# Slab 0's first weight columns tile by tile, gate and up in one slot: the head of a fused scan-and-GEGLU kernel re-ordered

## The chip, the cores and the metric

The kernel runs on one core of one Trainium2 chip. The metric is the device time of one execution in microseconds (us). Seven runs of the kernel before gave a median of 184.31 us, from 183.27 to 184.84: 183.27, 183.41, 183.49, 184.31, 184.45, 184.56 and 184.84. One execution was taken by the profiler; its own time was 183.49 us, and its span, from the first to the last instruction, 181.7 us.

Engines are called as the profile calls them: PE is the matrix engine, PEld its weight loads, DVE the vector engine, ACT the scalar engine, POOL the GpSimd engine, SP the sync engine. A "q" behind a name is that engine's DMA queue. An engine takes its instructions in the order in which the program lists them, and an instruction that waits holds up all those behind it on its engine.

## The reference, cut to what matters

```python
xn = layernorm(x)                               # x: 2048 tokens x 512
# branch A: a diagonal complex recurrence over the tokens
Lam_bar = exp(dt * Lam);  B_bar = ((Lam_bar - 1) / Lam)[:, None] * Bmat
h_t = Lam_bar * h_(t-1) + B_bar @ xn_t          # 512 complex states
s   = 2 * Re(h @ Cmat.T) + xn * Dskip
# branch B: gated feed-forward, 512 -> 1376 -> 512
g   = silu((gelu(xn @ w_gate) * (xn @ w_up)) @ w_down)
out = x + s * g
```

Inputs, weights and output are bfloat16.

## The kernel before, in words

The 2048 tokens are cut into four slabs of 512, each slab into four tiles of 128 (M = 4). The 1376 gate and up columns are cut into three chunks of 512, 512 and 352 (`CH`). PSUM is used as three slots of two banks (`slots[0..2]`, taken in turn by `slot()`) and two single banks (`ybank`).

Per slab the work is: layer norm of four tiles (`stats`, `rstd`, `norm_dve`: DVE makes the statistics, POOL the power -1/2, DVE the scaled tile `xn`); a transposition of `xn` to `xnT`; gate and up products on PE, moved out of PSUM by ACT (Gelu for gate, Copy for up) and multiplied on DVE into `at`; `half` twice (the products with B on PE, moved out by ACT into `U`, and then rotation, scan and back-rotation on DVE into `hst`); `down_pair` twice (the products with `w_down`); and `y_tile` four times (the products with C, then the end of the formula on DVE and a store).

Slab 0 is special. Its four tiles are transposed on PE through `ybank` and moved out by ACT (`head_t`, L642, `transposed`, L345), while later slabs use transposing DMAs (`dma_t`, L373). Its chunk 0 is done by `first_chunk` (L405): first the gate products of tiles 0 to 3 into two slots, then the up products of tiles 0 to 3 into two slots; ACT moves two tiles at a time (1024 columns). Chunks 1 and 2 of slab 0 use `gate_pair` (L384): one tile's gate and up share one slot, and ACT moves 512 or 352 columns at a time.

Before the first product, the program does the following. ACT's queue loads three small vectors of 512 (`pv0` = log_dt, `pv1` = Lambda_im, `pv2` = Lambda_re; L273) and then the gate weights of chunk 0. SP's queue loads the four x tiles, then the up weights of chunk 0, and chunk 1 and the rest. POOL's queue loads `Drow` (the row of Dskip). PE runs eight matmuls on a constant tile (`dummies`, L339), then `parameters` (L629): four tiny matmuls that turn `pv1`, `pv2`, `dt` and `dt*Lambda_im` into columns, and one that spreads `Drow` over 128 partitions, both into slot 2. ACT copies the spread row back (L637) and DVE copies the columns to `pf` (L638); since both share a slot, each waits for both. `tables` (L594) makes angles from `pf` on DVE (L598 to L602), their sines and cosines on ACT (L603, L604, then small copies on ACT and POOL, L606, L607) and the products of them on DVE (L618), from which the rotations are made.

The order on each engine is not written by hand. Each step is given to `Plan` (L23) with a cost, a lag until its result is seen elsewhere, what it reads and writes, and a rank. `Plan.run` (L113) makes a list schedule, repeats it with changed priorities, keeps the one with the best value, and then emits the steps in the order of their planned starts. PE's steps keep the order in which they were added. The plan only sets the order; the chip's time comes from the real waits.

Of the kernel before, what the change touches and what calls it, by code (L numbers as in the profile page):

```python
# [18 lines left out]
LOOK, HOLD, TABLE, ROUNDS, TRIALS = 0.3, 8.0, 6.0, 6, 1200  # L19
# [3 lines left out]
class Plan:  # L23
# [88 lines left out]

    def run(self):  # L113
        n = len(self.steps)
        deps = [s[3] for s in self.steps]
        users = [[] for _ in range(n)]
        for i in range(n):
            for d in deps[i]:
                users[d].append(i)
        tail = [0.0] * n  # L120
        for i in range(n - 1, -1, -1):
            eng, cost, lag = self.steps[i][0], self.steps[i][1], self.steps[i][4]
            tail[i] = cost + max((tail[u] + (0.0 if self._same(i, u) else lag) for u in users[i]), default=0.0)
        rank = [s[7] for s in self.steps]
        rng = random.Random(1)
        best = None
        prio = tail
        self.lengths = []
        work = [i for i in range(n) if self.steps[i][0] == PE]
        for r in range(ROUNDS + TRIALS):  # L130
            if r >= ROUNDS:
                lo = rng.uniform(-10.0, rng.choice((20.0, 170.0)))
                hi = lo + rng.choice((10.0, 25.0, 60.0))
                share, size = rng.choice((0.1, 0.3)), rng.choice((0.5, 2.0, 6.0))
                prio = [p + (rng.gauss(0.0, size) if lo <= t <= hi and rng.random() < share else 0.0) for p, t in zip(best[2], best[1])]
            key = [p + q for p, q in zip(prio, rank)]
            start, length = self._pass(deps, key, True)
            goal = length + 0.5 * sum(start[i] for i in work) / len(work)
            self.lengths.append(round(length, 1))
            if best is None or goal < best[0]:  # L140
                best = (goal, start, prio)
            if r < ROUNDS:
                back, _ = self._pass(users, [start[i] + self.steps[i][1] for i in range(n)], False)
                prio = [back[i] + self.steps[i][1] for i in range(n)]
        start = best[1]
        self.start = start
        for i in sorted(range(n), key=lambda i: (start[i], i)):
            self.steps[i][2]()
# [3 lines left out]
def kernel(  # L152
# [119 lines left out]
    for i, v in enumerate((A_log_dt, A_Lambda_im, A_Lambda_re)):  # L272
        dma_first(ACT, 0.45, 2.5, lambda i=i, v=v: nc.scalar.dma_start(out=pv[i][:], in_=v.rearrange("(k p) -> k p", p=P)),  # L273
            [("pv", i)], not_before=0.72)
    for m in range(M):
        dma_first(SP, 0.45, 1.75 + 0.12 * m, lambda m=m: nc.sync.dma_start(out=x_tok[:, m, :], in_=x_r[:, m, :]), [("x", 0, m)], not_before=0.72)
    load_w(dma_first, ACT, nc.scalar, 0, (0.47, 3.9), 0)
    for c, which, land in ((0, 1, 3.3), (1, 0, 3.1), (1, 1, 2.9)):
        load_w(dma_first, SP, nc.sync, c, (1.45, land), which)
    dma_first(SP, 1.45, 2.7, lambda: nc.sync.dma_start(out=x_tok[:, M : 2 * M, :], in_=x_r[:, M : 2 * M, :]), [("x", 1, m) for m in range(M)])  # L280
    for ri, src in enumerate((A_B_re, A_B_im)):
        dma_first(SP, 2.4, 2.7, lambda ri=ri, src=src: nc.sync.dma_start_transpose(out=BT[:, ri, :, :], in_=src), [("BT", ri)])
    for which in range(2):
        load_w(dma_first, SP, nc.sync, 2, (1.0, 2.7), which)
    ident = sb("ident", [P, P])
    id4 = sb("id4", [4, 4], FP32)
    pool(0.8, lambda: make_identity(nc, ident[:]), writes=["ident"], rank=190.0)
    dma(POOL, 0.7, 2.2, lambda: G.dma_start(out=Drow[0:1, :], in_=A_Dskip.rearrange("(a d) -> a d", a=1)), writes=["Drow"], rank=200.0)
# [18 lines left out]
    dve(128, lambda: V.tensor_tensor(out=pr[1][:], in0=pv[1][:], in1=pr[0][:], op=ALU.mult), [("pv", 1), "dtr"], ["thr"], base=0.13, rank=150.0)  # L307
# [37 lines left out]
    def transposed(src, n, dst, reads, writes, bank, evict):  # L345
        tp = ybank[bank][:].bitcast(BF16)[:, 0:D].rearrange("p (k t) -> p k t", t=P)

        def f():
            for k in range(KT):
                T.transpose(tp[:, k, :], src[:, k * P : (k + 1) * P], ident[:])  # L350
        pe(KT, P, f, reads + ["ident"], [("y", bank)])
        if evict == ACT:
            acts(512, lambda: act(out=dst, in_=tp, func=AF.Copy), [("y", bank)], writes, rank=40.0)
        else:
            dve(512, lambda: V.tensor_copy(out=dst, in_=tp), [("y", bank)], writes, rate=2.0, rank=40.0)
# [17 lines left out]
    def dma_t(s, m):  # L373
        c0 = (s % 2) * TS + m * P
        return dma(SP, 1.2, 1.3, lambda: nc.sync.dma_start_transpose(out=xnT[:, :, c0 : c0 + P], in_=xn[m][:]),
            [("xn", m)], [("xnT", s % 2, m)])
# [5 lines left out]
    gu_n = [0]  # L382

    def gate_pair(s, m, c):  # L384
# [9 lines left out]
        for bank, (nm, wt) in enumerate((("wg", wg), ("wu", wu))):  # L394
            def f(bank=bank, wt=wt):
                for k in range(KT):
                    T.matmul(ps[:, bank, 0:w], lhsT=xnT[:, k, t0 : t0 + P], rhs=wt[:, k, a:b], start=(k == 0), stop=(k == KT - 1))  # L397
            pe(KT, w, f, [("xnT", s % 2, m), (nm, c)], [("slot", i, bank)])
        both = [("slot", i, 0), ("slot", i, 1)]
        gd, ud = gt[qb][:, qo : qo + w], ub[qb][:, qo : qo + w]  # L400
        acts(w, lambda: act(out=ud, in_=ps[:, 1, 0:w], func=AF.Copy), both, [("ub", q)])
        acts(w, lambda: act(out=gd, in_=ps[:, 0, 0:w], func=AF.Gelu_apprx_tanh), both, [("gt", q)], table="gelu")
        dve(w, lambda: V.tensor_tensor(out=at[j][:, a:b], in0=gd, in1=ud, op=ALU.mult), [("gt", q), ("ub", q)], [("at", j, c)], rate=2.0)

    def first_chunk(between):  # L405

        w = CH[0][1]
        for nm, wt, dst, ring, fn in (("wg", wg, gt, "gt", AF.Gelu_apprx_tanh), ("wu", wu, ub, "ub", AF.Copy)):
            for h in range(2):
                i, ps = slot()  # L410
                for b in range(2):
                    m = 2 * h + b

                    def f(m=m, b=b, ps=ps, wt=wt):
                        for k in range(KT):
                            T.matmul(ps[:, b, :], lhsT=xnT[:, k, m * P : (m + 1) * P], rhs=wt[:, k, 0:w], start=(k == 0), stop=(k == KT - 1))  # L416
                    pe(KT, w, f, [("xnT", 0, m), (nm, 0)], [("slot", i, b)])
                    between(nm, m)
                both = [("slot", i, 0), ("slot", i, 1)]
                kw = {"table": "gelu", "after": early} if nm == "wg" else {}  # L420
                acts(2 * w, lambda ps=ps, dst=dst, fn=fn, h=h: act(out=dst[h][:, 0 : 2 * w].rearrange("p (b w) -> p b w", b=2), in_=ps[:, :, :], func=fn),
                     both, [(ring, 2 * h), (ring, 2 * h + 1)], **kw)
        for m in range(M):
            o = (m % 2) * w
            dve(w, lambda m=m, o=o: V.tensor_tensor(out=at[m][:, 0:w], in0=gt[m // 2][:, o : o + w], in1=ub[m // 2][:, o : o + w], op=ALU.mult),
                [("gt", m), ("ub", m)], [("at", m, 0)], rate=2.0)
# [165 lines left out]
    early = []  # L592

# [35 lines left out]
    def parameters():  # L629
        pt_ps = slots[2][:, 0, 0:16]  # L630
# [4 lines left out]
        pe(4, 150, f, [("pv", 1), ("pv", 2), "dtr", "thr", "ident", "id4"], [("slot", 2, 0)])  # L635
        pe(1, 512, lambda: T.matmul(slots[2][:, 1, :], lhsT=warm[0:1, 0:P], rhs=Drow[0:1, :], start=True, stop=True), ["Drow", "warm"], [("slot", 2, 1)])
        acts(512, lambda: act(out=Drow[:], in_=slots[2][:, 1, :], func=AF.Copy), [("slot", 2, 0), ("slot", 2, 1)], ["Drow"], rank=50.0)  # L637
        dve(16, lambda: V.tensor_copy(out=pf[:], in_=pt_ps), [("slot", 2, 0), ("slot", 2, 1)], ["pf", "thn", "dt"], rank=10.0)  # L638
# [5 lines left out]

    dummies(8, 0)
    parameters()
    dummies(2, 0)
# [5 lines left out]
    dummies(1, 1)  # L653
    head_t(1)

    def between(nm, m):
        if nm == "wg" and m + 2 < M:
            head_t(m + 2)
        if nm == "wg" and m == 0:
            tables()  # L660

    first_chunk(between)
    dma_first(SP, 3.6, 2.7, lambda: nc.sync.dma_start(out=wd[:, 0 : NFT - 1, :], in_=B_w_down[0 : (NFT - 1) * P, :].rearrange("(k p) d -> p k d", p=P)), ["wd"])
    dma_first(SP, 0.4, 2.7, lambda: nc.sync.dma_start(out=wd[:FL, NFT - 1, :], in_=B_w_down[(NFT - 1) * P : F, :]), ["wd"])
# [84 lines left out]
    for ri, src in enumerate((A_C_re, A_C_im)):  # L749
        dma(SP, 2.4, 2.7, lambda ri=ri, src=src: nc.sync.dma_start_transpose(out=CT[:, ri, :, :], in_=src),  # L750
# [69 lines left out]
```

## Time and profile before

| | |
|---|---|
| time, median of 7 runs (range) | 184.31 us (183.27 to 184.84) |
| time of the profiled execution; its span | 183.49 us; 181.7 us |
| PE busy | 174.7 us (96%) |
| DVE busy | 158.4 us (87%) |
| ACT busy | 118.2 us (65%) |
| POOL busy | 10.5 us (6%) |
| first gate matmul of slab 0 starts | 8.61 us |
| first matmul of chunk 1 starts | 16.41 us |
| last matmul ends, by the chain | 177.65 us |

The page gives, for one execution, the busy time of each engine, the chain of work that ended last, the costliest groups of instructions and the DMA issues. The chain is followed back from the last instruction, at each step to what released it. A timeline lists instructions in order of time: start, length, engine, line, operation, output and input; in brackets is the idle time of the engine before it and what ended that. A group in a timeline ("x4") runs from the start of its first to the end of its last. Ends of matmuls are modelled: four matmuls that are issued 0.22 us apart show as 1.03 us, because the last one is still draining while the next group has started.

### The profile page before, as it was taken

What the parts mean: (1) busy time and instruction counts of PE and PEld (TensorE: products, weight loads), DVE (VectorE), ACT (ScalarE), POOL (GpSimd) and SP (SyncE); (2) the same over time, 40 slices, a digit from 0 to 9 for tenths busy, and PEclk for the clock granted to TensorE, in tenths of its full rate; (3) what the DMA queues carried; (4) which work ended last, traced back from release to release, by engine and by line L of the source; (5) the groups of instructions that cost most, each with busy time, mean ns of one, the idle gap of its engine ahead of it and who ended that gap; (6) DMA issues with size and microseconds to landing.
All of it is one profiled execution on the core that took longest, in us unless ns stands there. A gap on an engine that the chain in (4) does not pass through costs nothing.

```text
span 181.7 us, 2385 instructions
## 1 busy us (share of the span) xinstructions
PE 174.7 (96%) x850; PEld 82.5 (45%) x850; DVE 158.4 (87%) x264; ACT 118.2 (65%) x174; POOL 10.5 (6%) x21
## 2 busy tenths in 40 slices
PE   6799999999999999999999999999999999999990
PEld 2444445544444545444444544544444545444440
DVE  5689999999999999999999999999999999740072
ACT  4578699799999899747349954527618666352220
POOL 4334002000000200000020000000000000000000
PEclk9999999999999999999999999999999999999998
DMA  4999999994000459500022470441100175720011
GB/s 116 370 316 227 356 125 209 283 192 106 0 0 0 87 101 140 108 0 0 19 69 61 94 141 10 79 79 61 39 21 0 23 89 92 146 81 8 0 58 58
DMA packets 46995, 18.01 MB, mean 99 GB/s; under 512 B 38440, under 2 KB 46984, under 8 KB 46984
## 3 DMA queue, kind: packets, MB, share of 16 engines
q1 hardware_dynamic: 46400, 17.34, 44.5%
q10 hardware_dynamic: 552, 0.53, 1.0%
q8 instruction: 6, 0.10, 0.2%
q14 instruction: 5, 0.04, 0.1%
q0 software_dynamic: 32, 0.00, 0.0%
HBM read 6.33 MB, written 2.10 MB: 46 GB/s over the span
## 4 chain that ended last, share of the span: by engine, by line
PE 54%; DVE 35%; ACT 6%; issue 3%; DVEq 0%
PE slot L440 18%; PE ybank L502 11%; PE slot L483 10%; DVE Fs L575 10%; DVE Q L556 9%; PE slot L542 6%; PE slot L397 4%; PE slot L342 2%; PE slot L416 2%; DVE C L758 2%; DVE at L458 1%; DVE hst L564 1%; DVE hst L568 1%; DVE C L755 1%; DVE sk L379 1%
## 5 line engine op out<-in xcount | busy, mean ns | idle before, releaser
L440 PEld LDWEIGHTS <-xnT 128*128 128x128 bf16 x288 | 28.1, 98 | 28.7 <-issue 0.3
L483 PE MATMUL slot<-wd,atT 128*128 128x512 bf16 (+1 forms) x176 | 38.7, 379 | 0.0
L440 PE MATMUL slot<-wg,xnT 128*128 128x512 bf16 (+1 forms) x144 | 31.8, 357 | 0.1
L440 PE MATMUL slot<-wu,xnT 128*128 128x512 bf16 (+1 forms) x144 | 31.8, 357 | 0.0
L575 DVE TENSOR_TENSOR_SCAN Fs<-rho,ini,W 128x512 bf16<-128x512 f32 x24 | 29.4, 1268 | 0.0
L502 PE MATMUL ybank<-C,hst 128*128 128x512 bf16 x128 | 28.8, 379 | 0.0
L542 PE MATMUL slot<-xnT,BT 128*128 128x512 bf16 x128 | 28.3, 379 | 0.0
L483 PEld LDWEIGHTS <-atT 128*128 128x128 bf16 (+1 forms) x176 | 17.2, 97 | 20.9
L545 ACT ACTIVATE U<-slot 128x1024 bf16<-128x1024 f32 x16 | 16.2, 1020 | 10.4 <-PE slot L542 10.2
L508 DVE TENSOR_TENSOR yg<-ybank,g 128x512 bf16<-128x512 f32 x14 | 9.6, 688 | 14.4 <-PE ybank L502 13.9
L542 PEld LDWEIGHTS <-BT 128*128 128x128 bf16 x128 | 12.5, 98 | 15.0
L502 PEld LDWEIGHTS <-hst 128*128 128x128 bf16 x128 | 12.5, 98 | 14.3
L556 DVE TENSOR_TENSOR Q<-U,tab 128x4096 bf16<-128x4096 bf16 x8 | 18.3, 2289 | 0.2
L556 DVE TENSOR_TENSOR Q<-Fs,tab 128x4096 bf16<-128x4096 bf16 x8 | 18.3, 2289 | 0.2
L498 ACT ACTIVATE ybank<-sk 128x512 f32<-128x512 bf16 x14 | 8.4, 601 | 15.2 <-DVE yg L508 14.7
L487 ACT ACTIVATE g<-slot 128x1024 f32<-128x1024 f32 x8 | 8.2, 1023 | 14.2 <-PE slot L483 14.1
L448 ACT ACTIVATE ub<-slot 128x1024 bf16<-128x1024 f32 x12 | 12.3, 1024 | 3.4 <-PE slot L440 3.4
L448 ACT ACTIVATE gt<-slot 128x1024 bf16<-128x1024 f32 x12 | 12.3, 1024 | 2.8 <-PE slot L440 2.8
L732 ACT ACTIVATE junk<-x_tok 128x512 bf16<-128x512 bf16 x16 | 10.0, 628 | 0.2
L575 DVE TENSOR_TENSOR_SCAN Fs<-rho,W 128x512 bf16<-128x512 f32 x8 | 9.4, 1209 | 0.0
L397 PEld LDWEIGHTS <-xnT 128*128 128x128 bf16 x64 | 6.3, 98 | 5.6
L458 DVE TENSOR_TENSOR at<-gt,ub 128x1024 bf16<-128x1024 bf16 x12 | 8.1, 677 | 0.0
(117 smaller groups left out, 183.8 us busy)
## 6 DMA issues: line engine op xcount, KB each, us to landing
out_dram<-ot SPq DMA_DIRECT2D x16, 128.0 KB, 1.7
x_tok<-in_A_x_dram SPq DMA_DIRECT2D x3, 512.0 KB, 7.2
wd<-in_B_w_down_dram SPq DMA_DIRECT2D x1, 1280.0 KB
wu<-in_B_w_up_dram SPq DMA_DIRECT2D x2, 512.0 KB
x_tok<-in_A_x_dram SPq DMA_DIRECT2D x4, 128.0 KB, 2.9
wg<-in_B_w_gate_dram ACTq DMA_DIRECT2D x1, 512.0 KB, 4.9
wg<-in_B_w_gate_dram SPq DMA_DIRECT2D x1, 512.0 KB, 6.5
wg<-in_B_w_gate_dram SPq DMA_DIRECT2D x1, 352.0 KB, 3.9
```

Of the source, the lines that this page charges most:

```text
L397: T.matmul(ps[:, bank, 0:w], lhsT=xnT[:, k, t0 : t0 + P], rhs=wt[:, k, a:b], start=(k == 0), stop=(k == KT - 1))
L440: T.matmul(ps[:, bank, 0 : b - a], lhsT=xnT[:, k, t0 : t0 + P], rhs=wt[:, k, a:b], start=(k == 0), stop=(k == KT - 1))
L448: acts(1024, lambda ps=ps, dst=dst, fn=fn: act(out=dst[:, 0:1024].rearrange("p (c w) -> p c w", c=2), in_=ps[:, :, :], func=fn), [("slot", ...
L458: dve(1024, lambda: V.tensor_tensor(out=at[j][:, 0:1024], in0=gt[q][:, 0:1024], in1=ub[q][:, 0:1024], op=ALU.mult), qs[0] + qs[1], [("at", ...
L483: T.matmul(ps[:, b, :], lhsT=atT[:fs, k, m * P : (m + 1) * P], rhs=wd[:fs, k, :], start=(k == 0), stop=(k == NFT - 1))
L502: T.matmul(bank[:, :], lhsT=hst[s % 2][:, j // NPT, j % NPT, m * P : (m + 1) * P], rhs=C2[:, j // NPT, j % NPT, :], start=(j == 0 and not ...
L508: dve(512, lambda: V.tensor_tensor(out=yg[e][:], in0=bank[:], in1=g2[gi][:, b, :], op=ALU.mult), [("y", i), ("g2", gi)], [("yg", e)])
L542: T.matmul(ps[:, ri, :], lhsT=BT[:, ri, k, pt * P : (pt + 1) * P], rhs=xnT[:, k, (s % 2) * TS : (s % 2 + 1) * TS], start=(k == 0), stop=(k ...
L545: acts(1024, lambda q=q, ps=ps: act(out=U[ui][:, :, q, :], in_=ps[:, :, :], func=AF.Copy), [("slot", i, 0), ("slot", i, 1)], [("U", ui, q)])
L556: dve(4096, lambda: V.tensor_tensor(out=Qf, in0=src.unsqueeze(1).to_broadcast(WQ), in1=table, op=ALU.mult), reads, ["Q"], rate=2.0)
L575: pl.add(DVE, 1.116 if s == 0 else 1.19, lambda ri=ri, q=q, pt=pt, first=first: V.tensor_tensor_scan(out=Fs[:, ri, q, :], data0=rho[:, pt ...
L732: acts(512, lambda i=i, fn=fn, m=m: act(out=junk[:], in_=x_tok[:, s * M + m, :], func=fn, accum_out=sx[:, s, i, m : m + 1]), [("x", s, m)] ...
```

## The change

In short: (1) `first_chunk` is gone. Chunk 0 of slab 0 is done by `gate_pair` like chunk 1: tile by tile, gate and up of a tile in one slot, moved out by ACT 512 columns at a time. The transpositions of tiles 1, 2 and 3 are put between these products: tile 1's behind gate 0, tile 2's behind up 0, tile 3's behind up 1. (2) `parameters` and the spreading of `Drow` (now `spread`) come behind the first transposed tile on PE instead of ahead of it, and write to slot 1 and slot 2, so that their copies no longer wait for each other. (3) Three of the eleven dummy matmuls are gone (the eight first ones stay). (4) `pv1` and `pv2` are loaded on POOL's queue instead of ACT's. (5) The assumed landing times of DMAs and some ranks are changed, and the planner has another search: `_decode` builds a schedule from a list of start times, and 3000 trials shift those. This changes the order on DVE and ACT in all of the kernel's first 100 us.

The order of the instructions that follows for each engine: PE: eight dummies, transposition 0, parameters, spread, gate 0, transposition 1, up 0, transposition 2, gate 1, up 1, transposition 3, gate 2, up 2, gate 3, up 3; from chunk 1 on as before. ACT, from its eighth instruction on: `xnT` of tile 0, `Drow`, `xnT` of tile 1, sine, copy, cosine, copy, `ub` 0, `xnT` of tile 2, the Gelu table, `gt` 0, `xnT` of tile 3, and then `ub`, `gt` of tiles 1, 2, 3. POOL: `Drow`'s load, the identity, the loads of `pv1` and `pv2`, the index rows (iota), three powers (tiles 0 to 2), two copies for the tables, the power of tile 3. DVE: statistics of tiles 0 and 1, `xn` 0, `dt*Lambda_im`, statistics of tile 2, `xn` 1, `pf`, three steps of the angles, `xn` 2, the fourth, statistics of tile 3, two products with `Drow`, `xn` 3. The set of DVE instructions ahead of the first rotation (L556 on `U0`) is the same in both. Further on, DVE makes slab 2's `sx` steps and `nb` (L737 to L743) ahead of two DVE steps of `y_tile` and three products with `Drow`, where they came behind them.

```diff
-    for i, v in enumerate((A_log_dt, A_Lambda_im, A_Lambda_re)):
-        dma_first(ACT, 0.45, 2.5, lambda i=i, v=v: nc.scalar.dma_start(out=pv[i][:], in_=v.rearrange("(k p) -> k p", p=P)),
-            [("pv", i)], not_before=0.72)
+    load_p(0, A_log_dt)
+    load_w(dma_first, ACT, nc.scalar, 0, (0.47, 4.5), 0)
...
+    for i, v in ((1, A_Lambda_im), (2, A_Lambda_re)):
+        dma(POOL, 0.7, 2.0, lambda i=i, v=v: G.dma_start(out=pv[i][:], in_=v.rearrange("(k p) -> k p", p=P)), writes=[("pv", i)], rank=220.0 - i, not_before=1.2)
...
-    def gate_pair(s, m, c):
+    def gate_pair(s, m, c, then=((), ())):
...
             pe(KT, w, f, [("xnT", s % 2, m), (nm, c)], [("slot", i, bank)])
+            for t in then[bank]:
+                head_t(t)
...
     def parameters():
-        pt_ps = slots[2][:, 0, 0:16]
+        pt_ps = slots[1][:, 0, 0:16]
...
-        pe(4, 150, f, [("pv", 1), ("pv", 2), "dtr", "thr", "ident", "id4"], [("slot", 2, 0)])
-        pe(1, 512, lambda: T.matmul(slots[2][:, 1, :], lhsT=warm[0:1, 0:P], rhs=Drow[0:1, :], start=True, stop=True), ["Drow", "warm"], [("slot", 2, 1)])
-        acts(512, lambda: act(out=Drow[:], in_=slots[2][:, 1, :], func=AF.Copy), [("slot", 2, 0), ("slot", 2, 1)], ["Drow"], rank=50.0)
-        dve(16, lambda: V.tensor_copy(out=pf[:], in_=pt_ps), [("slot", 2, 0), ("slot", 2, 1)], ["pf", "thn", "dt"], rank=10.0)
+        pe(4, 150, f, [("pv", 1), ("pv", 2), "dtr", "thr", "ident", "id4"], [("slot", 1, 0)])
+        dve(16, lambda: V.tensor_copy(out=pf[:], in_=pt_ps), [("slot", 1, 0)], ["pf", "thn", "dt"])
...
+    def spread():
+        pe(1, 512, lambda: T.matmul(slots[2][:, 1, :], lhsT=warm[0:1, 0:P], rhs=Drow[0:1, :], start=True, stop=True), ["Drow", "warm"], [("slot", 2, 1)])
+        acts(512, lambda: act(out=Drow[:], in_=slots[2][:, 1, :], func=AF.Copy), [("slot", 2, 0), ("slot", 2, 1)], ["Drow"])
+
     dummies(8, 0)
-    parameters()
-    dummies(2, 0)
...
     head_t(0)
-    dummies(1, 1)
-    head_t(1)
...
-    first_chunk(between)
+    parameters()
+    spread()
+    tables()
+    for m in range(M):
+        gate_pair(0, m, 0, (((1,), (2,)), ((), (3,)), ((), ()), ((), ()))[m])
```

## The prediction

> **What bounds the kernel now.** I read first the waits of PE, over the whole span; each line is: who waited for whom, us in total, times, longest.
>
> ```profile
> PE slot L342 <- DVE junk L297: 1.6, 1, 1.6
> PE ybank L350 <- DVE xn L369: 0.7, 1, 0.7
> PE slot L416 <- ACT gt L421: 0.3, 1, 0.3
> PE slot L416 <- ACT xnT L353: 0.2, 1, 0.2
> ```
>
> All of them lie before 15 us. From the first matmul of chunk 1 (16.41 us in the timeline) PE works without a hole that matters. I checked it by counting: 312 matmuls of 512 columns at 0.216 us (L542: 16 in 3.47 us) and 64 of 352 at 0.149 us (L397: 4 rows start 0.595 us apart) make 76.9 us, and 16.41 + 76.9 is 93.3, where slab 2's first gate matmul starts (93.33). So a change of the head can only move the time by what it moves chunk 1's start, plus stalls removed or made behind it. Second, the chain, in order of time, gives the head and the one later stall (start, length, what):
>
> ```profile
> 6.34 0.61 ACT Drow L637
> 6.97 0.17 DVE pf L638
> 7.14 0.33 DVE xn L369
> ...
> 7.52 0.41 PE ybank L350 x4
> 7.95 0.61 ACT xnT L353
> ...
> 8.61 1.04 PE slot L416 x4
> ...
> 12.31 1.28 ACT L421
> 13.61 1.03 ACT gt L421
> 14.68 1.89 PE slot L416 x8
> 16.57 6.91 PE slot L397 x32
> ...
> 95.07 0.81 ACT xn L714
> 95.90 1.28 ACT L448
> 97.20 1.03 ACT gt L448
> 98.27 4.81 PE slot L440 x24
> ```
>
> The reader sees the detour that the change removes: the first scaled tile waits on DVE behind `pf`, and `pf` behind the copy of `Drow`. At 98.27 PE had run out of work at 97.98 (4 up matmuls from 97.38, 0.149 each) and waited 0.29 us for a Gelu, which waited for a table, which waited for `xn`, which waited for `nb` on DVE. Third, busy time by stage: from 28.02 to 98.27 DVE is as full as PE.
>
> ```profile
> 28.02:98.27 70.25, 70.12 (x347) 33.79 (x346) 69.49 (x113) 56.75 (x90) 2.61 (x3) 1.00 0.45 87
> ```
>
> The columns are stage, length, then busy us and instructions of PE, PEld, DVE (69.49 of 70.25), ACT, POOL. A PE that starts earlier must find DVE earlier too.
>
> **The head, step by step.** POOL comes first, since the power for tile 0 now stands behind two more DMA issues. Rows of POOL:
>
> ```profile
> 1.21 0.73 POOL L288 DMA_DIRECT2D Drow<-in_A_Dskip_dram  x1 [0.78 <-POOLq L804]
> 2.60 0.18 POOL L289 CAST id<-ident 4x4 f32<-4x4 bf16 x1
> 2.74 0.15 POOL L312 IOTA iota_i<- 128x32 int32 x1
> 3.10 0.36 POOL L314 TENSOR_SCALAR iota_f<-iota_i 128x49 f32<-128x49 int32 x1
> 4.70 1.11 POOL L332 TENSOR_TENSOR rs<-ve,mhalf 128x1 f32<-128x1 f32 x2 [1.24 <-DVE mv L329]
> ```
>
> An issue of such a load on POOL is seen once, 0.73 us; two from 2.78 to 4.24, index rows 0.72 more (2.74 to 3.46 before), so the power runs 4.96 to 5.51 (0.55 each). The statistics of tile 0 are no obstacle (2.89 + 0.69 + 0.18 + 0.15, done at 3.96). `xn` 0: 5.56 to 5.96, against 7.06 to 7.46. The two issues are thus on the path; on ACT's queue such issues took 0.25 and 0.32. Bounds for the pair: 0.57 and 1.46; I take 1.46, the same queue. Drow's load landed 2.4 us after its issue began, so `pv2` lands at about 5.9; the slowest load in the head, 512 KB of x, took 7.8 us, which is the far bound.
>
> PE: transposition 0 at 6.02 (0.06 after `xn`, as before); its next group starts 0.23 us later; parameters and spread took from 5.09 to 6.23, 1.14 us, so gate 0 starts at 7.40 (its `xnT` is out at 7.07: ACT 0.60; gate weights landed 4.9 us after issue, so at about 6.3). Against 8.61 that is 1.2 us earlier. But ACT gives half of it back. Transposition 1 runs 8.27 to 8.66. ACT, with the start-to-start distances of the same rows: `xnT` 1 from 8.71 (0.50), sine (0.39), copy (0.22), cosine (0.48), copy (0.22), `ub` 0 at 10.52 (0.50), `xnT` 2 at 11.02 to 11.62, Gelu table 11.64 (1.28, +0.02), `gt` 0 at 12.94 (0.50), `xnT` 3 at 13.44 to 14.04. PE beside it: up 0 to 9.36, transposition 2, gate 1 and up 1 from 9.60 to 11.33; tile 3 waits for `xn` 3 (its power stands on POOL behind the two copies, the second from 10.30; 0.37 + 0.55, then DVE 0.40: 11.7), so transposition 3 at 11.75; gate 2 and up 2 from 12.0 to 13.72; gate 3 waits for `xnT` 3 and starts at 14.08; up 3 ends 15.81. Chunk 1 starts at **15.81 instead of 16.41: -0.60 us**. Its slot is free: `gt` 1 ends at 14.95.
>
> Costed at nothing: the three dummies (0.61 + 0.38 us of rows) lie in PE's waits for `xn` and `xnT`; the eight 512-wide evictions instead of four 1024-wide ones (0.50 x 8 against 1.03 x 4) run under chunk 1; the up weights, now needed at 8.5 instead of 12.5: by 6 us the load on SP's ring had moved 0.58 MB, of which 0.52 are x, so 0.46 MB is left at 370 GB/s and it ends near 7.3 to 7.9. If that cover of 0.6 us fails, each us costs a us.
>
> A rule of the Trainium skill speaks against the removed dummies. Row first: the eight dummies went at 0.45 us each, the spread at 5.93 took 0.37 us, which is the fast form; so PE's pace doubled between 5.16 and 5.93, while the granted clock in the stage rows stands at 1.00 throughout. "TensorE: Matmul & The Clock Gate", section "What's actually happening", says that the pace is set by how busy PE was in a free-running window of about 3.4 us. By it the hole from 5.16 to 6.02 might put off the fast form by a window in some executions; by the page's figure an estimate would be about 0.9 us more. No row here shows it.
>
> **Behind the head.** The same DVE set stands ahead of the first rotation. Its wait is ACT's `U`: ACT's last eviction of chunk 1 ends near 23.8, then a table copy (1.87) and two `U` (0.93, 1.02) make 27.6 instead of 28.02: DVE gains 0.4, PE 0.6. The tightest place behind it: `y_tile` 3 of slab 0 started at 75.19 and its bank was seeded at 75.00 (`ybank` L498, 74.40 + 0.60); this slack of 0.19 takes up the difference of 0.2. At 98 the order helps: `sx` comes ahead of two `y_tile` steps (0.35 and 0.69), so `nb` comes about 0.9 us earlier beside its 0.4, ACT's `xn` starts straight behind the Silu, and the Gelu ends 97.1 where PE needs its slot at 97.4. **-0.29 us**. From there PE is dense to 177.65 in both, and the tail is unchanged. Sum: -0.60 - 0.29 = -0.89. Against the profiled execution's own 183.49 that is 182.6; that execution lies 0.82 below the median of 184.31, to which the runs after will be compared, so **183.4**.
>
> **The rivals.** (A) *The gain is eaten.* DVE stays where it was, since `U` hangs on ACT's table copy, and PE waits for it at `y_tile` 3 and again at 98. For it: DVE's 99% between 28 and 98. Against: the first rotation does come earlier by the rows. It gives -0.2 to +0.4, so 184.1 to 184.7. (B) *Slower: POOL is the new link.* Tile 0 waits for a power behind two DMA issues, and parameters, gate 0 and all behind them wait for `pv2`. Each us that `pv2` lands past 6.2, or that the two issues last past 1.46, costs a us: nothing of the gain is left from 0.9 us on, that is a landing at 7.1, and slower by 0.5% from 1.8, a landing at 8.0. At 8.6 it is +1.5, 185.8. For it: the head's DMA engines are full from 5 us on, and x loads took 3.7 us in the middle. Against: Drow's 2.4 us on the same queue. (C) *More gain.* The issues cost 0.57 as on ACT's queue: the power is 0.9 earlier, `xn` 0 then waits for DVE's second statistics (4.76), transposition 0 comes at 5.3, 0.7 earlier: -1.6, 182.7; with no wait for tile 3 -2.0, 182.3.
>
> **How the numbers follow.** A measurement of this kernel can tell about 0.5%, 0.92 us, from no change: below 183.39 is faster, above 185.23 slower. Forecast 0.50 (183.4, own range 182.8 to 184.0), C 0.20, A 0.13, B 0.17. The forecast sits on the edge: half of it counts as faster, so faster 0.25 + 0.20 = 0.45; same 0.25 + 0.13 + 0.02 of B = 0.40; slower 0.15. The range takes in C's bound at the low side, 182.2, and B up to about a us, 185.3; what lies beyond is some 0.15 of B and C.
>
> **What would show it.** In the profile after: the power of tile 0 at 5.0, `xn` 0 at 5.6, gate 0 at 7.4, chunk 1 at 15.8, the first rotation near 27.6, no wait for a Gelu at 97, and PE's waits: one for `xn` 3 and one for `xnT` 3, about 0.4 us each. Wrong it would be if POOL's issues or the landing of `pv2` move gate 0, if early matmuls last 0.63 us each instead of 0.38 behind 6 us, or if PE shows a wait for DVE between 60 and 100.

## The result, and the profile after

The changed kernel took 185.97 us (median of 23 runs, 184.81 to 187.4) against 184.37 us of the kernel before (60 runs, 182.88 to 185.84). The ratio is 1.0101, with an interval from 1.0082 to 1.0121: slower by 1.0%. The profiled execution took 186.38 us, with a span of 184.6 us. Medians here are over all runs of a kernel; ratios leave out runs that took over 1.5% longer than the fastest of the same kernel, so the two can differ by some 0.3%.

First, PE's waits after, in the columns shown before (who waited for whom, us in total, times, longest):

```profile
PE slot L659 <- DMA pv<-in_A_Lambda_im_dram: 1.8, 1, 1.8
PE slot L389 <- DVE at L348: 1.6, 1, 1.6
PE ybank L397 <- DVE xn L416: 0.7, 1, 0.7
PE slot L659 <- DMA pv<-in_A_Lambda_re_dram: 0.4, 1, 0.4
```

The 1.6 is the start, as before. The waits for Gelu and for `xnT` are gone, and a new one stands at the top: the parameter matmuls (L659) wait for the two small loads that the change moved to POOL's queue, 2.2 us together. The chain of waits (start, length, what) names the same place:

```profile
2.83 0.49 POOL pv L334
3.32 4.96 DMA pv<-in_A_Lambda_re_dram
8.28 0.05 issue
8.32 1.08 PE slot L659 x5
9.40 0.45 PE slot L669
9.85 1.82 PE slot L445 x4
11.67 0.43 PE ybank L397 x4
12.10 1.71 PE slot L445 x4
```

A transfer of 1 KB holds the chain for 4.96 us. And behind it four matmuls of gate 0 last 1.82 us, which is 0.46 each in the chain (0.43 from start to start), twice the 0.216 of later ones. The stage rows show the granted clock in the third column from the end (stage, length, busy us of PE, PEld, DVE, ACT, POOL, clock, DMA share, GB/s):

```profile
5.16:8.00 2.84, 0.57 (x5) 0.32 (x5) 0.56 (x2) 0.60 (x1) 0.00 (x0) 0.99 1.06 344
8.00:10.00 2.00, 1.68 (x7) 1.15 (x8) 1.90 (x8) 0.11 (x1) 1.20 (x2) 0.50 1.08 380
10.00:12.00 2.00, 2.00 (x9) 0.99 (x8) 1.90 (x7) 0.48 (x1) 0.00 (x0) 0.50 1.27 324
12.00:14.00 2.00, 2.00 (x9) 0.90 (x8) 0.96 (x4) 1.80 (x6) 0.55 (x3) 0.50 1.04 234
```

PE was busy 0.57 of 2.84 us from 5.16 to 8.00; from 8 to 14 its clock stands at 0.50. In PE's timeline (start, length, engine, line, operation, operands, count) the pace comes back inside gate 1:

```profile
5.64 0.40 PE L397 MATMUL ybank<-ident,xn 128*128 128x128 bf16 x4 [0.68 <-DVE xn L416]
...
9.78 1.89 PE L445 MATMUL slot<-wg,xnT 128*128 128x512 bf16 x4
...
11.89 1.92 PE L445 MATMUL slot<-wu,xnT 128*128 128x512 bf16 x4
...
14.02 1.41 PE L445 MATMUL slot<-wg,xnT 128*128 128x512 bf16 x4
15.27 1.03 PE L445 MATMUL slot<-wu,xnT 128*128 128x512 bf16 x4
...
19.81 1.03 PE L445 MATMUL slot<-wg,xnT 128*128 128x512 bf16 x4
```

Transposition 0 at 5.64 was at full pace (0.40 for four); everything from the parameters to 14.8 was not. The last line is chunk 1, at 19.81 instead of 16.41, 3.40 later. Behind it the forecast held: 19.81 + 76.9 = 96.7, and slab 2's first gate matmul starts at 96.73; PE has no wait from 28 us to the end. So 3.40 were lost in the head. By the chain the last matmul ends at 180.80 instead of 177.63, 3.17 later, so some 0.23 was won back behind chunk 1, and the tail behind the last matmul was some 0.27 shorter. The execution itself was 2.89 longer (186.38 against 183.49). That is more than the 1.60 between the medians: the profiled execution of the kernel before lies 0.88 below its median, that of the changed kernel 0.41 above.

### The profile page after: what moved, and what is told of

It reads as the page before. It is cut to its first block, busy times and chain, and to the rows that moved or that the text cites. A ratio compares the mean times of both kernels' runs of the same rounds, so it can differ in the third digit from the quotient of the medians.

```text
span 184.6 us, 2392 instructions
## 1 busy us (share of the span) xinstructions
PE 176.4 (96%) x847; PEld 83.6 (45%) x847; DVE 159.2 (86%) x264; ACT 117.7 (64%) x178; POOL 10.5 (6%) x23
## 4 chain that ended last, share of the span: by engine, by line
PE 93%; DMA 3%; POOL 1%; DVE 1%; issue 0%; POOLq 0%
PE slot L467 30%; PE slot L510 21%; PE ybank L529 15%; PE slot L569 15%; PE slot L445 11%; DMA pv<-in_A_Lambda_re_dram 3%; PE slot L659 1%; PE ybank L397 1%; POOL Drow L335 0%; DVE yg L535 0%; POOL pv L334 0%; PE slot L669 0%; DVE ot L543 0%; POOL ident masks.py:199 0%; POOL ident masks.py:197 0%
## 5 line engine op out<-in xcount | busy, mean ns | idle before, releaser
L467 PEld LDWEIGHTS <-xnT 128*128 128x128 bf16 x288 | 28.1, 98 | 28.4
L467 PE MATMUL slot<-wg,xnT 128*128 128x512 bf16 (+1 forms) x144 | 31.8, 357 | 0.0
L467 PE MATMUL slot<-wu,xnT 128*128 128x512 bf16 (+1 forms) x144 | 31.8, 357 | 0.0
L445 PEld LDWEIGHTS <-xnT 128*128 128x128 bf16 x96 | 9.7, 103 | 9.7 <-issue 2.1
L445 PE MATMUL slot<-wg,xnT 128*128 128x512 bf16 (+1 forms) x48 | 12.5, 387 | 0.0
L445 PE MATMUL slot<-wu,xnT 128*128 128x512 bf16 (+1 forms) x48 | 12.1, 378 | 0.0
```

The source lines that it names most:

```text
L467: T.matmul(ps[:, bank, 0 : b - a], lhsT=xnT[:, k, t0 : t0 + P], rhs=wt[:, k, a:b], start=(k == 0), stop=(k == KT - 1))
```

## The experiments

Two theories stood. **L (landing):** the two loads on POOL's queue land late, PE waits, and the hole also costs it its full pace. **O (order):** the new order itself, tile by tile with the parameters behind the first tile, makes the head longer, and the loads only show up as the wait that comes last. All kernels keep the order on each compute engine of the kernel they start from, but for what the diff adds, takes out or moves. Ratios are to runs of the kernel before on the same chip, with medians of 184.41 (28 runs, first four) and 184.59 (29 runs, last four). The profiled executions of e2, e3 and e7 were the longest of their runs (185.15, 185.16 and 185.06 us), that of e6 the longest but one (185.25), so their rows tell what can happen in these kernels, and the medians what it is worth.

**e1: the two loads back on ACT's queue, the rest of the change kept.**

```diff
     def load_p(i, v):
-        dma_first(ACT, 0.4, 2.3, lambda: nc.scalar.dma_start(out=pv[i][:], in_=v.rearrange("(k p) -> k p", p=P)), [("pv", i)], not_before=0.72)
+        def f():
+            for j, u in ((i, v), (1, A_Lambda_im), (2, A_Lambda_re)):
+                nc.scalar.dma_start(out=pv[j][:], in_=u.rearrange("(k p) -> k p", p=P))
+        dma_first(ACT, 0.4, 2.3, f, [("pv", i)], not_before=0.72)
...
-        dma(POOL, 0.7, 2.0, lambda i=i, v=v: G.dma_start(out=pv[i][:], in_=v.rearrange("(k p) -> k p", p=P)), writes=[("pv", i)], rank=220.0 - i, not_before=1.2)
+        dma(POOL, 0.7, 2.0, lambda: None, writes=[("pv", i)], rank=220.0 - i, not_before=1.2)
```

> The changed kernel with the loads of Lambda_im and Lambda_re put back on ACT's queue, ahead of the gate weights, as they were before; the order on every engine is that of the changed kernel. Theory (these two loads land at 7.8 and 8.3 us on POOL's queue, PE stands idle for them and then runs at half pace): both are there before the first transposition is done, gate 0 starts near 6.7, its matmuls last 0.38 us, chunk 1 starts between 15.0 and 15.9, and the time is 182.4 to 183.5. Rival 1 (the tile-by-tile order with its 512-wide evictions and the Gelu table in the middle is what costs): chunk 1 stays behind 17 and the time above 185. Rival 2 (the three missing dummies let PE's pace fall by themselves): gate 0 is early, but its matmuls last 0.63 us and the time is 184 to 185.

Measured: 183.03 us, ratio 0.9924 [0.9888, 0.9959]. It is faster than the kernel before, by 0.8%, and than the changed one. PE's only wait is the start, and its timeline reads:

```profile
5.21 0.61 PE L400 MATMUL ybank<-ident,xn 128*128 128x128 bf16 x4
5.75 0.21 PE L662 MATMUL slot<-ident,pv 4*128 4x4 bf16 x2
5.82 0.99 PE L662 MATMUL slot<-id,pr 4*128 4x4 f32 x4
6.68 0.58 PE L672 MATMUL slot<-Drow,junk 1*128 1x512 bf16 x1
7.19 1.89 PE L448 MATMUL slot<-wg,xnT 128*128 128x512 bf16 x4
...
16.59 1.03 PE L448 MATMUL slot<-wg,xnT 128*128 128x512 bf16 x4
```

The parameters follow the first tile without a hole, and gate 0 starts 2.59 us earlier than in the changed kernel. O falls: the new order wins once the loads are in time. One thing isn't as expected: gate 0 again lasts 1.89 us, at half pace, though PE never stood still. That is the sign of rival 2, at a time (183.41 in this execution) that is not rival 2's; no run puts the three dummies back. The half pace also ate the early start of this execution: chunk 1 starts at 16.59, where the profile before had 16.41. So the gain of e1 is shown by its runs, and its profile does not show where it lies.

**e2: the changed kernel, with ten matmuls on the constant tile in the hole.** They run between transposition 0 and the parameters.

```diff
         def f():
+            for _ in range(10):
+                T.matmul(slots[0][:, 0, :], lhsT=warm[:, 0:P], rhs=warm[:], start=True, stop=True)
```

> The changed kernel with ten dummy matmuls on slot 0 between the first transposition and the parameters, so that PE is at work while it waits for the loads; nothing else moves. Theory (late landing and half pace are two separate terms): the loads still land near 7.8 and 8.3 and gate 0 still starts at 9.4 to 9.8, but no matmul behind 6 us lasts 0.63 us; chunk 1 starts near 18.0 instead of 19.98, and the time is 184.3 to 185.2. Rival 2 (only the pace matters): the loss is gone, below 184.0. Rival 1 (the order costs): no change, near 186.

Measured: 184.2 us, ratio 0.9992 [0.9964, 1.002]. In this profiled execution (185.15) the load landed even later, at 9.38, and still chunk 1 started at 18.61, 1.2 earlier than in the changed kernel. From PE's waits and its timeline:

```profile
PE slot L661 <- DMA pv<-in_A_Lambda_re_dram: 1.1, 1, 1.1
```

```profile
5.87 2.32 PE L659 MATMUL slot<-junk 128*128 128x512 bf16 x10
...
10.27 1.04 PE L445 MATMUL slot<-wg,xnT 128*128 128x512 bf16 x4
...
18.61 1.03 PE L445 MATMUL slot<-wg,xnT 128*128 128x512 bf16 x4
```

Ten useless matmuls kept the pace: gate 0 takes 1.04 instead of 1.89, and from gate 0 to chunk 1 it is 8.34 us instead of 10.03. PE still stood idle for 1.1 us in the middle and kept the pace. So 1.7 us of the loss is the pace and not the landing. By the ratios (times 184.4) the changed kernel stands at +1.86, e2 at -0.15, e1 at -1.40: filling the hole is worth 2.0 us, and the loads in time 1.25 more.

**e3: the loads stay on POOL's queue but are issued first, ahead of `Drow` and the identity.**

```diff
-        dma(POOL, 0.7, 2.0, lambda i=i, v=v: G.dma_start(out=pv[i][:], in_=v.rearrange("(k p) -> k p", p=P)), writes=[("pv", i)], rank=220.0 - i, not_before=1.2)
-    dma(POOL, 0.7, 2.2, lambda: G.dma_start(out=Drow[0:1, :], in_=A_Dskip.rearrange("(a d) -> a d", a=1)), writes=["Drow"], rank=200.0)
+        dma(POOL, 0.7, 2.0, lambda: None, writes=[("pv", i)], rank=220.0 - i, not_before=1.2)
+    def small_loads():
+        for i, v in ((1, A_Lambda_im), (2, A_Lambda_re)):
+            G.dma_start(out=pv[i][:], in_=v.rearrange("(k p) -> k p", p=P))
+        G.dma_start(out=Drow[0:1, :], in_=A_Dskip.rearrange("(a d) -> a d", a=1))
+
+    dma(POOL, 0.7, 2.2, small_loads, writes=["Drow"], rank=200.0)
```

> The changed kernel with the two loads still on POOL's queue, but issued as POOL's first work, ahead of Drow's load and of the identity (issue near 1.25, 1.8 and 2.35 instead of 2.78, 3.32 and, for Drow, 1.25). If the queue needs about 5 us from issue to landing whenever: landings near 6.3, 6.8 and, for Drow, 7.3; gate 0 about a us earlier than in the changed kernel, and 184.5 to 185.3. If the landing is set by the big loads that fill the DMA engines (it comes when the gate and x loads are through): landings near 7.8 as before and about 186. If an early issue on this queue lands in 2.4 us as Drow's did before the change: gate 0 near 7.5 and about 183.5.

Measured: 183.4 us, ratio 0.9917 [0.9884, 0.995], much like e1. The loads landed at about 5.5 and 6.6 (issued at 1.27 and 2.03), and PE waited 0.3 us for them. Only the landings are used of this profile. The queue may stay; an issue 1.3 to 1.5 us earlier is enough. On the way these loads took 4.2 and 4.6 us, not much less than the 5.0 of the changed kernel. So the landings are those of the first case above and the time is that of the third: e3 alone does not tell whether the queue or the traffic makes the load slow. e5 does.

**e4: the kernel before, with nothing changed but that the two loads are issued on POOL's queue behind the identity.**

```diff
-        dma_first(ACT, 0.45, 2.5, lambda i=i, v=v: nc.scalar.dma_start(out=pv[i][:], in_=v.rearrange("(k p) -> k p", p=P)),
+        dma_first(ACT, 0.45, 2.5, lambda i=i, v=v: i or nc.scalar.dma_start(out=pv[i][:], in_=v.rearrange("(k p) -> k p", p=P)),
...
-    pool(0.25, lambda: G.tensor_copy(out=id4[:], in_=ident[0:4, 0:4]), ["ident"], ["id4"], rank=190.0)
+    def id4_loads():
+        G.tensor_copy(out=id4[:], in_=ident[0:4, 0:4])
+        for i, v in ((1, A_Lambda_im), (2, A_Lambda_re)):
+            G.dma_start(out=pv[i][:], in_=v.rearrange("(k p) -> k p", p=P))
+
+    pool(0.25, id4_loads, ["ident"], ["id4"], rank=190.0)
```

> The kernel before with one part of the change alone: the loads of Lambda_im and Lambda_re on POOL's queue, behind the identity as in the changed kernel, with the order of the kernel before on every engine. Theory: the product dt*Lambda_im on DVE and the parameters on PE wait for landings near 7.8 and 8.3, and since DVE's product stands ahead of the statistics' second half and pf ahead of xn 0, the first gate matmul comes at 11.5 to 12.5 instead of 8.61, with PE at half pace for some us: 187 to 189. Rival 1 (the order of the changed kernel costs, not the queue): near the time before, 184.0 to 185.

Measured: 187.81 us (four runs), ratio 1.0181 [1.0147, 1.0214]: this one edit costs 1.8%. The same waits appear in the old order, and here nearly all of the hole is in one piece:

```profile
PE slot L639 <- DMA pv<-in_A_Lambda_im_dram: 2.9, 1, 2.9
```

**e5: why so late? The changed kernel, with the large weight loads held until the first scaled tile is written.** The two small loads keep their queue and place. The gate weights come late in this kernel, so its time (187.67, one run) says nothing of the change; only the landings are read.

```diff
+    def hold(emit, cell):
+        if free:
+            emit()
+        else:
+            held.append((emit, cell))
+
+    def release():
+        free.append(1)
+        for _, cell in held:
+            V.memset(cell, 0.0)
+        for emit, _ in held:
+            emit()
...
-        put(eng, *land, lambda w=w, r=r: q.dma_start(out=w[:, :, a:b], in_=r[:, :, a:b]), writes=[(nm, c)], **kw)
+        put(eng, *land, lambda w=w, r=r: hold(lambda: q.dma_start(out=w[:, :, a:b], in_=r[:, :, a:b]), w[:, 0, a : a + 2]), writes=[(nm, c)], **kw)
...
-            op0=ALU.subtract, op1=ALU.mult), [("x", s, m), ("mv", s, m), ("rs", s, m)], [("xn", m)], rate=2.0)
+            op0=ALU.subtract, op1=ALU.mult), (s, m) == (0, 0) and release()), [("x", s, m), ("mv", s, m), ("rs", s, m)], [("xn", m)], rate=2.0)
```

> The changed kernel with the big weight loads (gate and up, chunks 0 and 1, and what stands behind them on SP's queue) held back until xn 0 is written, near 5.6 us; three tiny writes on DVE do the holding. It is slower by construction (gate 0 waits for weights until 10 or later); only the landing of POOL's three loads is read from it. If the DMA engines' load of big transfers makes the landing late: Lambda_im and Lambda_re land 2.2 to 3.2 us after their issue, near 5.2 and 6.0, instead of 7.8 and 8.3. If the queue itself takes about 5 us for the second and third load: still 7.5 or later.

Measured, in the DMA issues (the last number is us from issue to landing), the changed kernel first and e5 second:

```profile
Drow<-in_A_Dskip_dram POOLq DMA_DIRECT2D x1, 1.0 KB, 4.2
pv<-in_A_Lambda_im_dram POOLq DMA_DIRECT2D x1, 1.0 KB, 5.0
pv<-in_A_Lambda_re_dram POOLq DMA_DIRECT2D x1, 1.0 KB, 5.0
```

```profile
Drow<-in_A_Dskip_dram POOLq DMA_DIRECT2D x1, 1.0 KB, 2.3
pv<-in_A_Lambda_im_dram POOLq DMA_DIRECT2D x1, 1.0 KB, 1.8
pv<-in_A_Lambda_re_dram POOLq DMA_DIRECT2D x1, 1.0 KB, 1.6
```

The same loads on the same queue, issued at the same 2.78 and 3.32 us, land after 1.8 and 1.6 us when the weights, and what stands behind them on SP's queue, are not on their way. So it is this traffic that makes them late; the queue by itself does not. The stages from 2.8 to 3.9 and from 3.9 to 8.3 us, changed kernel first and e5 second, have the DMA share as their last number but one and GB/s as the last:

```profile
2.80:3.90 1.10, 1.10 (x4) 0.45 (x3) 0.98 (x4) 1.07 (x4) 1.09 (x4) 1.00 0.84 172
3.90:8.30 4.40, 1.63 (x9) 0.47 (x7) 1.69 (x7) 1.65 (x3) 1.15 (x5) 0.96 1.07 354
```

```profile
2.80:3.90 1.10, 1.10 (x4) 0.45 (x3) 1.03 (x4) 1.08 (x3) 1.09 (x4) 1.00 0.84 253
3.90:8.30 4.40, 3.39 (x15) 1.61 (x14) 3.61 (x16) 1.78 (x4) 2.35 (x6) 1.00 0.31 65
```

Up to 3.9 us the engines of e5 are no quieter. Then the x tiles are in: from 3.90 to 4.95 they move 11 GB/s, and the two loads land at 4.58 and 4.92. In the changed kernel the weights run at 354 GB/s from there on, and the loads land at 7.8 and 8.3.

"DMA: Bandwidth & Descriptors", section "Anatomy of one DMA — SWDGE (gpsimd) path", in the Trainium skill gives such a load a fixed cost of about 2.0 us plus its bytes. The 1.6 to 2.3 us of e5 agree with that; the 5.0 us beside the weights do not, and there the measurement decides.

**e6: the loads on SP's queue, behind the four x tiles.**

```diff
-        dma_first(eng, 0.45, land, lambda: q.dma_start(out=x_tok[:, m, :], in_=x_r[:, m, :]), [("x", 0, m)], not_before=0.72)
+        dma_first(eng, 0.45, land, lambda: (q.dma_start(out=x_tok[:, m, :], in_=x_r[:, m, :]), m == M - 1 and small_loads()), [("x", 0, m)], not_before=0.72)
+
+    def small_loads():
+        for i, v in ((1, A_Lambda_im), (2, A_Lambda_re)):
+            nc.sync.dma_start(out=pv[i][:], in_=v.rearrange("(k p) -> k p", p=P))
...
-        dma(POOL, 0.7, 2.0, lambda i=i, v=v: G.dma_start(out=pv[i][:], in_=v.rearrange("(k p) -> k p", p=P)), writes=[("pv", i)], rank=220.0 - i, not_before=1.2)
+        dma(POOL, 0.7, 2.0, lambda: None, writes=[("pv", i)], rank=220.0 - i, not_before=1.2)
```

> The changed kernel with the two loads on SP's queue behind the four x tiles, issued near 2.6 and 2.9, so at the same moment as on POOL's queue (2.78, 3.32) and into the same traffic. If POOL's queue is what makes them late: they land before 6.0, PE waits for them less than 0.3 us, and the time is within 0.6 of the one with ACT's queue (183.03). If the moment is what makes them late, whichever the queue: near 7.5 and 185 to 186.

Measured: 183.82 us, ratio 0.9953 [0.9908, 0.9998]. Issued at 2.6 and 3.0 us, they were awaited by PE until 6.46 (`PE slot L663` waited 0.7 us), so some 3.8 us from issue to use: late on this queue too. It lies between e1 and the changed kernel, as its landing does, and fits neither expectation in full: the wait is longer than 0.3 us, and the landing is earlier than 7.5. On SP's queue the load took some 1.2 us less than on POOL's. No run tells whether that is the queue or the traffic, since the up weights, which stand behind the two loads on SP's queue, are issued 0.7 us later here (3.29 instead of 2.59).

**e7: the other half of the change by itself. The kernel before, with the parameters in another slot's bank, so that `pf` no longer waits for the copy of `Drow`.**

```diff
-        pt_ps = slots[2][:, 0, 0:16]
+        pt_ps = slots[1][:, 1, 0:16]
```

> The kernel before with one part of the change alone: the parameters go to a bank of another slot, so that the copy pf no longer waits for Drow's copy; all orders are those of before. By my working of the detour: pf at 6.1 instead of 6.97, xn 0 done near 6.6 instead of 7.46, the first transposition at 6.85 behind the two dummies, gate 0 near 7.9 instead of 8.61, chunk 1 0.2 to 0.7 earlier: 183.7 to 184.2 against 184.4. Rival (the Gelu table and the order of evictions end the first chunk anyway): no change that can be measured.

Measured: 183.83 us, ratio 0.9967 [0.994, 0.9993]. A gain of 0.6 us, for one line. In its profile, which is of its longest run, the scaled tile comes early, and the next thing is late: PE waits for the gate weights, and then it too has lost its pace.

```profile
PE slot L416 <- DMA wg<-in_B_w_gate_dram: 1.3, 1, 1.3
```

```profile
6.36 0.40 PE L350 MATMUL ybank<-ident,xn 128*128 128x128 bf16 x4
...
8.52 1.86 PE L416 MATMUL slot<-wg,xnT 128*128 128x512 bf16 x4 [1.33 <-DMA wg<-in_B_w_gate_dram]
```

Four transposing matmuls took 0.40 ahead of the hole of 1.33 us, and four gate matmuls 1.86 behind it, the time of eight at full pace (1.89).

**e8: e1, with the spreading of `Drow` and its copy moved behind gate 0,** to bring gate 0 forward by the 0.5 us that the spread takes.

```diff
+                if (s, m, c, bank) == (0, 0, 0, 0):
+                    T.matmul(slots[2][:, 1, :], lhsT=warm[0:1, 0:P], rhs=Drow[0:1, :], start=True, stop=True)
+                    act(out=Drow[:], in_=slots[2][:, 1, :], func=AF.Copy)
...
-        pe(1, 512, lambda: T.matmul(slots[2][:, 1, :], lhsT=warm[0:1, 0:P], rhs=Drow[0:1, :], start=True, stop=True), ["Drow", "warm"], [("slot", 2, 1)])
-        acts(512, lambda: act(out=Drow[:], in_=slots[2][:, 1, :], func=AF.Copy), [("slot", 2, 0), ("slot", 2, 1)], ["Drow"])
+        pe(1, 512, lambda: None, ["Drow", "warm"], [("slot", 2, 1)])
+        acts(512, lambda: None, [("slot", 2, 0), ("slot", 2, 1)], ["Drow"])
```

> The version with ACT's queue for the loads (183.03) with one more move: the matmul that spreads Drow, and its copy on ACT, come behind gate 0 instead of ahead of it, since Drow is needed later than gate 0. At the fast pace the spread takes 0.45 us of PE between 6.8 and 7.26, and gate 0 could start at 6.8 when its weights land. Theory: 0 to 0.4 us faster than 183.03. Rival (ACT's chain of evictions, sines and the Gelu table ends the first chunk): no change.

Measured: 183.65 us, ratio 0.9952 [0.9918, 0.9987], not better than e1. Gate 0 started at 7.03 instead of 7.19, because PE now waited 0.3 us for the gate weights. In e7 and e8 the next limit of gate 0 is thus its weights, not its tile.

## Why the prediction was wrong, step by step

**The step that failed is the landing of `pv2`.** The prediction put it at about 5.9, from the 2.4 us of `Drow`'s load in the profile before. It was 8.28, 4.96 us after its issue. The row was of the same queue but not of the same moment: `Drow` was issued at 1.21 us and had landed at 3.6, in stages where the DMA engines moved 113 and 212 GB/s (1.2 to 2.4 and 2.4 to 3.6 us). The moved loads were issued at 2.78 and 3.32 and had to land while the weights ran at 354 GB/s. The change also brought that traffic forward: with two issues less on ACT's queue the gate weights are issued at 1.32 instead of 1.93, and from 3.6 to 4.8 us the engines move 341 GB/s instead of 184. Even `Drow`'s own load, issued at 1.25, took 4.2 us there instead of 2.4. e5 shows that this traffic is the cause, and e4 that the two loads alone are enough to make the kernel before slower. The prediction named the traffic as what speaks for rival B ("the head's DMA engines are full from 5 us on") and let the wrong row outweigh it. Both signs of being wrong that it named for this case came: the landing moved gate 0, and early matmuls behind 6 us went at half pace.

**The price of the landing was nearly right, the price of the hole was missing.** By B each us past 6.2 costs a us: 8.28 makes 2.08, and gate 0 came 2.38 late (9.78 instead of 7.40); the 0.3 between is the tiny matmuls and the spread at half pace (1.08 + 0.45 in the chain, against 1.14). Then from gate 0 to chunk 1 it took 10.03 us where the forecast had 8.41: 1.62 of pace, which e2 gives back (8.34). The sum closes for the two profiled executions: 182.6 + 2.38 + 1.62 = 186.6, measured 186.38; the 0.2 left over is about what the tail was shorter. Between the medians the miss is smaller, 185.97 against 183.4, and no profile of a middle run splits it. B was the case that came true, with 0.17 against 0.50 for the forecast. Its own time at 8.28 would have been 184.31 - 0.89 + 2.08 = 185.5, against the median of 185.97.

**The rule on the clock, set aside.** The prediction quoted "TensorE: Matmul & The Clock Gate", section "What's actually happening", for the hole from 5.16 to 6.02 and put nothing into the sum for it. Here the granted clock is 0.50 from 8 to 14 us behind a hole of 1.8 us, and e2 takes it away by filling the hole. So this case agrees with the page in kind, that the pace follows how busy PE was. The page has the half rate come after an idle window of about 3.4 us; here a hole of 1.8 us was enough (2.9 in e4, 1.3 in e7), and there the measurement decides. One of 1.1 us in e2 cost nothing. In size it was 1.6 to 1.7 us, where the estimate from the page's window was 0.9; a whole window of 3.4 us at half pace gives 1.7, an estimate too. Here it was two such lengths, with PE idle in part of them: by finer rows the granted clock stood at 0.50 for 6.8 us in the changed kernel (7.96 to 14.79) and in e4 (7.66 to 14.49), and for 3.4 us in e7 (8.54 to 11.95), once that length.

**What held.** POOL's two issues were on the path, but took 0.55 and 0.50 instead of twice 0.73, so the power ran at 4.56 instead of 4.96, `xn` 0 at 5.17 instead of 5.56 and transposition 0 at 5.64 instead of 6.02: part of rival C's head start did come. DVE's order held up nothing behind chunk 1: from 28.02 to 98.27 PE is busy all the time. That does not yet put rival A out, since chunk 1 came 3.40 later, and in e1, where PE had no wait behind the start either, 0.18 later than before; no profile here has it earlier.

```profile
28.02:98.27 70.25, 70.25 (x347) 33.75 (x346) 69.12 (x115) 56.75 (x90) 2.11 (x2) 1.00 0.42 86
```

The stall for a Gelu at 98 is gone, the forecast's -0.29: between chunk 1 and the last matmul some 0.23 of the 3.40 came back. And e1 shows what the change is worth with the loads in time: -0.76%, or -1.4 us, where the forecast said -0.9. This bears out its sign and not its steps, since the profile of e1 has chunk 1 at 16.59 and not at 15.81.

**A wait that the prediction did not follow.** DVE's product on `pv1` (L354) stood behind the same landing and idled DVE for 2.27 us; the last step of the statistics of tile 1 stood behind it, so POOL's second power began at 8.29. The prediction named only PE behind `pv2`. In e2, where PE kept its pace, this shows: transposition 3 waited 0.36 for `xn`.

**Open.** In e1 the first matmuls ran at half pace to about 10.6 us without a hole, and in the profile before PE was at full pace from 5.9 on. The granted clock reads 1.00 in both. e8, e6 and e3 are like e1, with the full pace from about 10.6, 13.6 and 14.0 us on: there transposition 0 took 0.61 us, so PE had not yet reached it, while in the changed kernel (0.40) it had, and lost it. No run here tells what decides it, or whether the three removed dummies have a part in it; the runs of e1 lie between 181.78 and 185.51, those of e2 between 183.83 and 185.15. The 24 runs of the changed kernel (23 and the profiled one) differ too: six have a mean granted clock of 0.98 (186.38 to 187.40 us, the profiled one the fastest of them), six of 0.99 (184.81 to 185.56) and twelve of 1.00 (185.48 to 186.20), and all are above the median of the kernel before. The loss of pace behind a hole is shown (e2 against the changed kernel); the moment at which the pace returns is not explained. Nor was it tried which of the weight loads delays the small ones: `Drow`'s load before landed after 2.4 us though the DMA share was 1.04 from 2.4 to 3.6 us, so full engines alone do not set the price.

## What to carry to other kernels

A small load takes its price more from the traffic while it is under way than from its queue or its size: take a row of the same moment and the same traffic, ask whether the change itself moves that traffic, or issue the load ahead of the large ones (e1 and e3 are two ways). A wait on PE in the head can have two prices, its length and the half pace behind it; a few useless matmuls in the hole pay for the second one. And when an operation is moved to where it waits, look for every engine that stands behind the same landing.

## What the runs showed of the hardware that was not expected

On POOL's queue a load of 1 KB landed after 1.6 to 1.8 us where the DMA engines fell quiet meanwhile (e5, 11 GB/s) and after 4.2 to 6.1 us beside weight loads (e2, e3, e4 and the changed kernel; 319 to 360 GB/s from 5.16 to 8.00 us); on SP's queue it was not usable before about 3.8 us (e6). The half clock behind a hole came in lengths of 3.4 us, once (e7) or twice (e4 and the changed kernel). The record of the granted clock is no proof of pace: in e1 it reads 1.00 from 8 to 10 us, while four 512-column matmuls take 1.89 us instead of 1.03. Useless matmuls can make a kernel faster: ten of them, 2.32 us of PE time, made the changed kernel 2.0 us faster by the ratios.
